# Short dummy matmuls at the start, one relu moved up, and the third batch's q scaled earlier in a fused attention and expert kernel

## The chip, the cores and the metric

The kernel runs on one core of one Trainium2 chip. The metric is the device time of one execution in microseconds (us), the median over several executions. Profiles are single executions; their clock starts at the first instruction of the program.

## The reference

```python
q_p = concat([relu(q) * cos, relu(q) * sin], -1)     # the same for k; cos and sin by position
kv  = einsum('bhsf,bhsd->bhfd', k_p, v); z = k_p.sum(2)
x   = einsum('bhsf,bhfd->bhsd', q_p, kv) / (einsum('bhsf,bhf->bhs', q_p, z) + 1e-6)
# x is laid out as 4608 x 512. Gates: exp(x @ w_gate), balanced 8 times over rows and columns
for e in range(8):
    out += P[:, e:e+1] * (relu(x @ w1[e]) @ w2[e])
```

There are 8 batches of 8 heads, 576 positions and 64 columns per head. Each expert is 512 by 1024 and 1024 by 512.

## The kernel before

The first phase works in blocks. Block j multiplies 512 tokens by the first expert's weights, slot by slot (slots 0 to 7 the first matrix, 8 to 15 the second). Between the slots it prepares the attention of a batch ahead: block 0 finishes batch 1 and starts batch 2 ("the third batch"), block 1 finishes batch 2, and so on. A helper, `at(block, slot, function, ...)`, puts a piece of work behind a slot. Three engines matter here: PE (TensorE), DVE (VectorE) and ACT (ScalarE). In these traces a piece that waits holds up what is written behind it on that engine: the k_p behind DVE's fourth scaling starts at 54.45 us in before, behind a wait of 1.91 us, and the first of four at 54.74 in after, behind one of 7.94 us (timelines below).

The parts that matter, abridged (`...` marks cuts):

```python
ld      = ...tile_pool(name="ld", bufs=4)        # loads of q, k, v: four half batches each
qp_pool = ...tile_pool(name="qp_pool", bufs=3)   # scaled q: three buffers

def keep_busy(n):                                # n * 128 columns of matmuls whose result is not used
    for cols in [512] * (n // 4) + [n % 4 * 128] * (n % 4 > 0):
        te.matmul(out=idle_ps[:, 0:cols], lhsT=ones_sq[:], rhs=..., start=True, stop=True)

def prep_q(b, hk):                               # two heads of batch b
    q16 = loaded.pop(("q", b, hk))
    if b >= 2: ve.tensor_scalar(out=q16, in0=q16, ..., op0=ALU.max)       # DVE relu
    q_p = qp_pool.tile([P, C, 2, D], F16, name="q_p")
    ve.tensor_tensor(out=q_p[:], in0=q16..., in1=cs, op=ALU.mult)         # DVE scaling
    if b >= 2:                                                            # turned by a DMA
        nc.sync.dma_start(out=qTs[b, hk], in_=q_p[:]..., transpose=True)
# prep_k: relu of k on ACT (b > 0); prep_kp: k_p, on DVE; prep_v: copy of v
# sums: k_p.T @ v on PE; denominators: PE, needs all four turned q; attend: the division
...
for hk in range(HK):                             # before block 0
    attend(0, hk)
    ...                                          # matmuls of slots 0 to 3, and for hk == 3 four relus on ACT
    for i in ((), (0,), (1, 2), (3,))[hk]: prep_k(1, i)
    for i in ((), (0,), (1,), (2, 3))[hk]: prep_kp(1, i)
...
# batch 2, as written: slots 12 to 15 of block 0, then slots 0, 1 and 3 of block 1
(12, prep_q, 0), (12, prep_k, 0), (13, prep_q, 1), (13, prep_k, 1),
(14, prep_kp, 0), (14, prep_v, 0, se.copy), (15, prep_kp, 1), (15, prep_v, 1, se.copy),
...
for hk in (2, 3):
    at(j, 0, prep_q, b, hk); at(j, 0, prep_k, b, hk)
    at(j, hk - 2, prep_kp, b, hk); at(j, hk - 2, prep_v, b, hk, se.copy)
at(j, 1, sums, b, 0); at(j, 3, sums, b, 1)
...
at(0, 3, load, 2, half); at(1, 0, load, 3, half)   # loads: the queue runs ahead of the slots
```

With three buffers for scaled q, the fourth scaling of a batch takes the buffer of its first. It waits until the first transposing DMA has landed (1.91 us in before; in b_bufs4, with a fourth buffer, not at all).

The softmax here doesn't subtract the row's maximum and nothing guards it: scores larger than these inputs give would overflow.

## Time and profile before

| what | before |
|---|---|
| time, median | 986.65 us (986.33 to 986.86, 4 runs) |
| first matmul of block 1 / of block 2 (timeline) | 48.03 us / 72.33 us |
| first transposing DMA: issued, landed | 46.09 us, 53.68 us |
| last load of batch 3 landed (trace record) | 52.65 us |

The page begins with the span and each engine's busy time and share:

```profile
span 985.4 us, 20168 instructions
## 1 busy us (share of the span) xinstructions
PE 967.8 (98%) x7817; PEld 671.3 (68%) x7817; DVE 805.8 (82%) x1829; ACT 566.7 (58%) x1267; POOL 60.6 (6%) x82
```

PE is nearly full, so what can be won are its holes. The view of waits for PE, from 8 to 75 us, says whom it waited for: total in us, how often, the longest.

```profile
PE small_ps L109 <- DVE k_p L109: 1.7, 1, 1.7
PE small_ps L109 <- DVE q_p L109: 1.6, 1, 1.6
PE small_ps L109 <- DMA q_pT<-q_p: 1.1, 1, 1.1
PE small_ps L109 <- issue: 0.9, 1, 0.9
PE h_ps L109 <- ACT hT L109: 0.6, 1, 0.6
```

"issue" means that nothing in the profile explains the wait. The chain that ended last, followed back through 40 to 62 us, has a start, a length and what was waited for on each line:

```profile
46.09 7.58 DMA q_pT<-q_p
53.68 0.03 issue
...
53.77 0.77 DVE q_p L109
...
54.62 4.59 DMA q_pT<-q_p
```

So the chain goes through the first transposing DMA, then the fourth scaling, then that one's own DMA. DVE's timeline (start, length, operation, and in brackets the idle time before it) shows the waiting instruction with its neighbours:

```profile
50.89 0.75 DVE L109 TENSOR_TENSOR k_p<-k_ld,acc_hi 128x1152 f16<-128x1152 f16 x1
51.56 0.30 DVE L109 TENSOR_SCALAR q_ld<-q_ld 128x576 f16<-128x576 f16 x1
53.77 0.76 DVE L109 TENSOR_TENSOR q_p<-q_ld,acc_hi 128x1152 f16<-128x1152 f16 x1 [1.91 <-DMA q_pT<-q_p]
54.45 0.75 DVE L109 TENSOR_TENSOR k_p<-k_ld,acc_hi 128x1152 f16<-128x1152 f16 x1
```

The last view is the table of busy time by stretch: busy us (and count) of PE, PEld, DVE, ACT and POOL, then the granted TensorE clock, DMA share and GB/s.

```profile
49.00:55.00 6.00, 3.98 (x67) 1.85 (x64) 4.05 (x8) 4.96 (x11) 0.00 (x0) 1.00 1.25 175
55.00:58.00 3.00, 2.75 (x44) 1.56 (x45) 0.85 (x5) 1.72 (x5) 0.00 (x0) 1.00 1.19 120
58.00:61.00 3.00, 1.90 (x37) 1.11 (x31) 1.33 (x2) 1.15 (x3) 0.00 (x0) 1.00 0.05 9
```

### The profile page before, as it was taken

The page shows a single profiled execution, that of the slowest core. Times are in us where ns is not written, and L with a number is a line of the kernel's source. Part 1 is how long each engine was busy: PE and PEld are TensorE (multiplying, and loading weights), DVE is VectorE, ACT ScalarE, POOL GpSimd, SP SyncE. Part 2 cuts the span into 40 slices and gives each one's busy share as a digit, 9 for nine tenths or more (in the row PEclk, how much of TensorE's full clock was granted, in tenths as well). Part 3 has the DMA queues.
Part 4 walks back from the last instruction along what each step waited for, and adds up shares of the span by engine and source line. Part 5 has one row for each costly group of instructions (what it writes and reads, how often), then busy time and mean ns, then how long its engine had stood idle before and what let it go on. Part 6 is the DMA issues. An engine that isn't in the chain of part 4 may idle for free.

```text
span 985.4 us, 20168 instructions
## 1 busy us (share of the span) xinstructions
PE 967.8 (98%) x7817; PEld 671.3 (68%) x7817; DVE 805.8 (82%) x1829; ACT 566.7 (58%) x1267; POOL 60.6 (6%) x82
## 2 busy tenths in 40 slices
PE   9889999989999999999999999999999999999997
PEld 4444544447777777777777777777777777777775
DVE  6676774789889888988789888988788888988887
ACT  5666665467776555555555555555555555555551
POOL 6311110010000000000000000000000000000001
PEclk9999999999999999999999999999999999999999
DMA  9979990641013410133103400233103401104435
GB/s 163 206 115 158 158 155 13 131 76 54 33 42 68 83 33 26 42 75 67 50 25 69 91 25 25 52 65 68 49 26 68 91 25 30 44 25 118 127 87 128
DMA packets 80336, 73.54 MB, mean 75 GB/s; under 512 B 33264, under 2 KB 72176, under 8 KB 80240
## 3 DMA queue, kind: packets, MB, share of 16 engines
q0 software_dynamic: 27232, 30.94, 19.9%
q1 hardware_dynamic: 52768, 41.06, 17.1%
q8 instruction: 61, 1.00, 0.4%
q14 instruction: 35, 0.29, 0.1%
q10 hardware_dynamic: 240, 0.26, 0.1%
HBM read 83.12 MB, written 12.98 MB: 98 GB/s over the span
## 4 chain that ended last, share of the span: by engine, by line
PE 94%; DVE 2%; ACT 2%; DMA 1%; issue 0%; POOL 0%; SPq 0%; ACTq 0%; DVEq 0%; POOLq 0%
PE rows_ps L109 34%; PE h_ps L109 27%; PE copied_ps L109 11%; PE p_ps L109 11%; PE y_ps L109 6%; PE small_ps L109 4%; DMA q_pT<-q_p 1%; ACT hT L109 0%; DVE acc_hi L904 0%; POOL hs_last L919 0%; DVE P_tok L109 0%; DMA out_dram<-acc_lo 0%; DVE colp L109 0%; ACT u L109 0%; ACT acc_lo L109 0%
## 5 line engine op out<-in xcount | busy, mean ns | idle before, releaser
L904 DVE SCALAR_TENSOR_TENSOR acc_lo<-rows_ps,P_tok,acc_lo 128x512 f32<-128x512 f32 (+1 forms) x322 | 203.9, 643 | 74.5 <-PE rows_ps L109 74.4
L109 PEld LDWEIGHTS <-H 128*128 128x128 f16 x2080 | 203.0, 98 | 83.1 <-issue 1.2
L840 ACT CAST u<-h_ps 128x384 f16<-128x384 f32 x288 | 137.6, 478 | 131.3 <-PE h_ps L109 131.3
L109 PEld LDWEIGHTS <-w1e 128*128 128x128 f16 x1632 | 156.4, 98 | 67.2 <-issue 6.9
L834 DVE CUSTOM_DVE_ANT_0 H<-p_ps,u 128x384 f16<-128x384 f32 x329 | 181.9, 553 | 7.0 <-PE p_ps L109 6.3
L109 PEld LDWEIGHTS <-hs 128*128 128x128 f16 x1500 | 146.5, 98 | 56.2
L109 PE MATMUL h_ps<-S,w1e 128*128 128x384 f16 x672 | 164.1, 326 | 1.1 <-ACT u L109 0.9
L109 PE MATMUL p_ps<-xT,T 128*128 128x384 f16 x672 | 164.1, 326 | 0.1
L109 PE MATMUL h_ps<-xT,w1e 128*128 128x384 f16 (+1 forms) x616 | 150.1, 350 | 0.8 <-ACT hT L109 0.6
L109 PE MATMUL rows_ps<-V,H 128*128 128x256 f16 x1000 | 150.0, 273 | 0.7 <-DVE acc_hi L904 0.7
L109 PE MATMUL rows_ps<-w2e,hs 128*128 128x256 f16 x1000 | 150.0, 273 | 0.0
L872 ACT ACTIVATE H<-h_ps 128x384 f16<-128x384 f32 x144 | 70.6, 490 | 95.1 <-PE h_ps L109 95.1
L109 PEld LDWEIGHTS <-T 128*128 128x128 f16 x1008 | 98.1, 98 | 29.3 <-issue 2.8
L109 PE MATMUL rows_ps<-w2e,H 128*128 128x256 f16 (+1 forms) x568 | 91.2, 285 | 0.0
L853 ACT COPY copied_ps<-h_ps 128x384 f32<-128x384 f32 x144 | 67.5, 469 | 35.3 <-PE h_ps L109 35.3
L863 ACT ACTIVATE H<-copied_ps 128x384 f16<-128x384 f32 x144 | 70.8, 492 | 20.4 <-PE copied_ps L109 20.4
L109 PE MATMUL h_ps<-S,T 128*128 128x384 f16 x336 | 81.8, 325 | 0.3 <-ACT copied_ps L109 0.3
L109 PE MATMUL copied_ps<-xT,w1e 128*128 128x384 f16 x336 | 82.1, 326 | 0.0
L109 PE MATMUL copied_ps<-w2e,H 128*128 128x256 f16 x504 | 75.5, 272 | 0.0
L109 PE MATMUL rows_ps<-V,hs 128*128 128x256 f16 x500 | 75.0, 272 | 0.0
L904 DVE SCALAR_TENSOR_TENSOR acc_lo<-copied_ps,P_tok,acc_lo 128x256 f32<-128x256 f32 x126 | 60.4, 480 | 0.4
L904 DVE SCALAR_TENSOR_TENSOR acc_hi<-rows_ps,P_tok,acc_hi 128x512 f32<-128x512 f32 (+1 forms) x56 | 41.4, 739 | 19.9 <-PE rows_ps L109 19.1
(147 smaller groups left out, 952.4 us busy)
## 6 DMA issues: line engine op xcount, KB each, us to landing
S<-x_saved SPq DMA_DIRECT2D x108, 192.0 KB, 2.4
out_dram<-acc_lo SPq DMA_DIRECT2D x62, 128.0 KB, 2.4
w1e<-in_moe_w_dram POOLq DMA_DIRECT2D x7, 1024.0 KB, 9.0
w2e<-in_moe_w_dram POOLq DMA_DIRECT2D x7, 1024.0 KB, 10.1
q_ld<-in_q_dram POOLq DMA_DIRECT2D x16, 288.0 KB, 7.5
k_ld<-in_k_dram POOLq DMA_DIRECT2D x16, 288.0 KB, 8.9
v_ld<-in_v_dram POOLq DMA_DIRECT2D x16, 288.0 KB, 9.4
x_saved<-S SPq DMA_DIRECT2D x18, 192.0 KB, 1.9
```

What stands on the lines that cost most here:

```text
L109: i = getattr(self.engine, name)(*args, **kwargs)
L834: latest = ve._custom_dve(TENSOR_ADD_SAT, out=out, in0=ps[:, 0:TU], in1=t[:], s0=FP32_MAX, s1=0.0)
L840: se.copy(out=t[:], in_=ps[:, 0:TU])
L853: se.copy(out=Y[:, 0:TU], in_=X[:, 0:TU])
L863: se.activation(out=h11, in_=Y[:, 0:TU], func=AF.Relu)
L872: se.activation(out=h12, in_=X[:, 0:TU], func=AF.Relu)
L904: ve.scalar_tensor_tensor(out=a, in0=rows, scalar=P_tok[:, g, self.e : self.e + 1], in1=a, op0=ALU.mult, op1=ALU.add,)
```

## The change

There are three parts, to which the rest of this text refers.

- *Dummies*: the first 80 dummy units are issued as 80 matmuls of 128 columns instead of 20 of 512.
- *Relu*: ACT's relu of k(1,3) stands ahead of four relus of the expert's hidden layer, so that k_p and q_p of batch 1 come sooner.
- *Order*: all four scalings of batch 2's q move into block 0 (from slot 8 on), so that their transposing DMAs start sooner. The keys and values of batch 2 follow as the first work of block 1, and its attends start at slot 9.

```diff
-        keep_busy(80)
+        for _ in range(80):
+            keep_busy(1)
@@
-        def prep_k(b, hk):
+        def prep_k(b, hk, by_scalar=True):
-            if b:
+            if b and by_scalar:
@@
             attend(0, hk)
+            if hk == 3:
+                prep_k(1, 3)
@@
-            for i in ((), (0,), (1, 2), (3,))[hk]:
+            for i in ((), (0,), (1, 2), ())[hk]:
                 prep_k(1, i)
@@  block 1
-                    for hk in (2, 3):
-                        at(j, 0, prep_q, b, hk)
-                        at(j, 0, prep_k, b, hk)
-                        at(j, hk - 2, prep_kp, b, hk)
-                        at(j, hk - 2, prep_v, b, hk, se.copy)
-                    at(j, 1, sums, b, 0)
-                    at(j, 3, sums, b, 1)
+                    for hk in range(HK):
+                        if hk >= 2:
+                            at(j, 0, prep_k, b, hk, False)
+                        at(j, 0, prep_kp, b, hk)
+                        at(
+                            j, (0, 0, 1, 3)[hk], prep_v, b, hk,
+                            (ve.tensor_copy, se.copy)[hk // 2],
+                        )
+                    at(j, 3, sums, b, 0)
+                    at(j, 5, sums, b, 1)
@@
-                at(j, 5 if j == 1 else 3, denominators, b)
+                at(j, 6 if j == 1 else 3, denominators, b)
                 for hk in range(HK):
-                    at(j, (8 if j == 1 else 6) + 2 * hk, attend, b, hk)
+                    at(j, (9, 10, 12, 13)[hk] if j == 1 else 6 + 2 * hk, attend, b, hk)
@@  block 0
-                    (12, prep_q, 0), (12, prep_k, 0), (13, prep_q, 1), (13, prep_k, 1),
-                    (14, prep_kp, 0), (14, prep_v, 0, se.copy), (15, prep_kp, 1),
-                    (15, prep_v, 1, se.copy),
+                    (8, prep_q, 0), (11, prep_k, 0), (12, prep_q, 1), (12, prep_k, 1),
+                    (13, prep_q, 2), (14, prep_q, 3),
```

(The slots of batch 3's preparation in block 1 are rearranged too; that list is cut here.)

## The prediction

> **What bounds the kernel now.** The page gives PE 967.8 of 985.4 us busy (98%), and the chain that ended last is 94% PE: time can only come from where PE stands still. The change touches the first 72 us. The table by stretch shows PE full from 60 to 180 us, but not before (6.62 of 10 us in 50 to 60). The timeline shows PE's holes:
> - 30.15 us: 1.6 us, transposes of batch 1 wait for q_p; DVE had waited 2.46 us for ACT's relu of k(1,3), queued behind four hidden relus.
> - 34.0 and 34.6 us: 0.32 and 0.21 us; ACT is nearly full there.
> - 52.1 us: 0.57 us (ACT hT); 55.26: 1.70 us (k_p of batch 2); 59.25: 1.10 us (last transposing DMA). The chain of waits has 7.58 us DMA q_pT from 46.09, a DVE q_p, then 4.59 us DMA q_pT: with three q_p buffers the fourth scaling waits for the first transpose.

> **Parts, costed.**
> 1. 80 dummies of 128 columns for 20 of 512: same columns. Weight loads come 0.42 us apart until 6.24 us, then about 0.21. [...] That moment should stay; with more weight loads (nine warm 128-column pairs took 0.68 us) the dummies end 0.2 to 0.6 us later. Keys land at 10.7 us anyway. Cost 0 to 0.3 us.
> 2. ACT's k(1,3) before the four relus: k_p and q_p of batch 1 come 2 us earlier, the 1.6 us hole closes, then ACT limits. Gain 1.3 us.
> 3. Batch 2's q from slot 8 (DVE idles near 41 us): first transpose 5 us earlier, no 4.59 us tail. The 3.4 us of holes close in part. Given back: block 1 starts with about 4.4 us of DVE work (two relus 0.30, four k_p 0.75, two copies 0.45) behind the last q_p; the sums at slot 3 need v(2,1): PE waits 0.5 to 1.8 us. DMA is saturated till 52 us (205 GB/s), so the first transpose may take 7 us again and hold the fourth scaling 1.5 us. DVE has about 21 us of work in block 1 against PE's 20.2: 0.3 to 0.8 us of wait moves to batch 3's sums. Net gain 1.5 us.

> From 60 us PE is full, and later holes (180 to 220 us, sinkhorn) follow work that moves along: the gain is kept.

> **Prediction.** 986.6 - 1.3 - 1.5 + 0.1 = 983.9 us; 8 in 10: 981.8 to 986.3. Faster by over 2%: 0.01; within 2%: 0.98; slower by over 2%: 0.01.

> **What would show each step right.**
> - Dummies: first transposes at 8.7 to 9.1 us (before 8.54), first DVE zsel at most 0.3 us after 12.39.
> - k(1,3): q_p of batch 1 starts near 27 us (before 29.34), no PE wait for it; sums of batch 1 1 to 1.5 us earlier.
> - First transposing DMA at 40 to 42 us (before 46.09), last landed before 58 (59.2); PE's waits in 48 to 60 us 1 to 2.5 us, on k_p or v of batch 2.
> - Block 2's first matmuls 2 to 3.5 us earlier (before 72.33), everything later shifted the same.

> **What would make it wrong.** If transposes starve behind the loads, the fourth q_p blocks DVE 4 us or more: no gain, or a loss. If short dummies leave the array cold longer, the start loses 1 us or more. If neither, and DVE keeps up, the gain is 4 to 5 us. The compiler may also order loads differently.

## The result

The changed kernel takes 990.04 us (989.82 to 990.27, 4 runs) against 986.65 us. The ratio is 1.0035, with a 95% interval of 1.0017 to 1.0052. Ratios here are the mean time of one kernel's fast runs over that of the other's of the same rounds, so they are not quite the ratio of the quoted medians. The change is a loss of 3.4 us, clear of noise, and the time lies outside the predicted range.

```profile
span 988.3 us, 20283 instructions
## 1 busy us (share of the span) xinstructions
PE 969.5 (98%) x7877; PEld 676.3 (68%) x7877; DVE 807.0 (82%) x1833; ACT 565.3 (57%) x1263; POOL 60.6 (6%) x82
```

The page hardly differs; the loss is in one place. PE's waits from 8 to 75 us:

```profile
PE small_ps L109 <- DVE acc_lo L109: 7.6, 3, 6.9
PE small_ps L109 <- ACT acc_lo L109: 0.2, 1, 0.2
PE small_ps L109 <- ACT acc_hi L109: 0.2, 1, 0.2
PE h_ps L109 <- DVE xT L109: 0.2, 1, 0.2
```

The waits for q_p, k_p, the DMA and "issue" that were listed before are gone. In their place stands one hole of 6.9 us. (The name acc_lo here is the space that is lent to the copies of v.) The chain from 40 to 62 us shows what is behind it:

```profile
39.69 14.29 DMA q_pT<-q_p
...
54.07 0.76 DVE q_p L109
54.83 0.67 DVE k_p L109
55.49 0.36 DVE acc_lo L109
55.86 0.67 DVE k_p L109
56.52 0.37 DVE acc_lo L109
```

The first transposing DMA was issued 6.4 us sooner than before, at 39.69 instead of 46.09. It landed at 53.97, which is 0.3 us later than before. DVE's timeline shows the cost:

```profile
45.83 0.30 DVE L109 TENSOR_SCALAR q_ld<-q_ld 128x576 f16<-128x576 f16 x1
54.07 0.76 DVE L109 TENSOR_TENSOR q_p<-q_ld,acc_hi 128x1152 f16<-128x1152 f16 x1 [7.94 <-DMA q_pT<-q_p]
54.74 0.75 DVE L109 TENSOR_TENSOR k_p<-k_ld,acc_hi 128x1152 f16<-128x1152 f16 x1
```

The fourth scaling waited 7.94 us instead of 1.91, and now all four k_p of batch 2 stand behind it. The table by stretch has a second effect in its column of clocks (the seventh after the stretch's length):

```profile
49.00:55.00 6.00, 0.00 (x0) 0.00 (x0) 0.93 (x2) 1.16 (x2) 0.00 (x0) 0.91 1.25 187
55.00:58.00 3.00, 1.74 (x38) 1.31 (x39) 2.97 (x7) 0.38 (x2) 0.00 (x0) 0.50 0.66 132
58.00:61.00 3.00, 3.00 (x10) 0.91 (x10) 2.12 (x6) 0.66 (x2) 0.00 (x0) 0.54 0.00 0
```

While PE stood idle the array's clock was halved, and it stayed halved after work came back. The trace's clock record has one spell of 6.83 us at 0.5 there (53.96 to 60.78 us), and none there in before. PE's hole is 6.94 us (48.97 to 55.91).

The balance, from the two timelines: block 1 starts 2.71 us earlier (45.32 instead of 48.03), and block 2 starts 3.05 us later (75.38 instead of 72.33). So block 1 takes 5.76 us more. After 75 us PE's larger holes (over 0.25 us) add up to 4.24 us in before and in after: the later parts neither gave nor took.

### The profile page after: what moved, and what is told of

Its sections match the earlier page's. It is cut to its first block, busy times and chain, and to the rows that moved or that the text cites. A ratio compares the mean times of both kernels' runs of the same rounds, so it can differ in the third digit from the quotient of the medians.

```text
span 988.3 us, 20283 instructions
## 1 busy us (share of the span) xinstructions
PE 969.5 (98%) x7877; PEld 676.3 (68%) x7877; DVE 807.0 (82%) x1833; ACT 565.3 (57%) x1263; POOL 60.6 (6%) x82
## 3 DMA queue, kind: packets, MB, share of 16 engines
q1 hardware_dynamic: 52768, 41.06, 16.9%
## 4 chain that ended last, share of the span: by engine, by line
PE 93%; DVE 2%; ACT 2%; DMA 2%; POOL 0%; issue 0%; ACTq 0%; SPq 0%; DVEq 0%; POOLq 0%
PE rows_ps L109 34%; PE h_ps L109 27%; PE copied_ps L109 11%; PE p_ps L109 11%; PE y_ps L109 6%; PE small_ps L109 4%; DMA q_pT<-q_p 1%; ACT hT L109 0%; DVE acc_hi L913 0%; POOL hs_last L928 0%; DVE P_tok L109 0%; DMA out_dram<-acc_lo 0%; DVE colp L109 0%; ACT u L109 0%; ACT acc_lo L109 0%
```

## The experiments

Two theories of the transposing DMA were set against each other.

- *Drain theory*: issued while loads are queued, it lands only when those loads have drained, near 54 us, whenever it was issued.
- *Own-time theory*: it takes its time from its issue (7.6 us before, 14.3 us after), so a later issue means a later landing.

Of the gains in front there was a second pair: *additive* (an earlier start of block 1 is kept, as I had predicted) against drain (it is swallowed by a landing that does not move).

The twelve new kernels gave correct results, and every one was run with a profile and in three timed rounds beside the kernel before on the same chip. Landings are the trace's own records, in us. The column of loads gives the last landing of the loads that are in flight with the transpose. In after, b_filled, b_q3_after_keys and b_bufs4 the last of these was issued 0.5 to 1.2 us behind the transpose (at 40.84 in after), in the other runs ahead of it.

| kernel | time, median | ratio (95% interval) | first transpose: issued, landed | last load landed | DVE wait at 4th scaling |
|---|---|---|---|---|---|
| before (profile) | 986.65 | | 46.09, 53.68 | 52.65 | 1.91 |
| after (profile) | 990.04 | 1.0035 (1.0017 to 1.0052) | 39.69, 53.97 | 53.96 | 7.94 |
| a_dummies | 987.02 | 0.9999 (0.9984 to 1.0014) | 45.65, 52.22 | 51.07 | 0.89 |
| a_relu | 987.63 | 1.0009 (0.9994 to 1.0023) | 44.04, 53.30 | 52.52 | 3.58 |
| a_dummies_relu | 988.72 | 1.0020 (1.0005 to 1.0035) | 43.92, 55.24 | 53.04 | 5.64 |
| a_order | 989.51 | 1.0027 (1.0010 to 1.0044) | 42.27, 53.33 | 52.85 | 4.82 |
| b_q0_late | 989.20 | 1.0024 (1.0009 to 1.0039) | 43.86, 53.05 | 52.27 | 5.68 |
| b_q3_after_keys | 985.54 | 0.9989 (0.9973 to 1.0006) | 39.63, 54.82 | 54.86 | 4.83 |
| b_filled | 988.80 | 1.0021 (1.0006 to 1.0036) | 38.87, 53.59 | 53.69 | 8.37 |
| b_loads_held | 983.40 | 0.9968 (0.9951 to 0.9984) | 39.47, 44.39 | 43.18 (batch 2's) | none |
| b_bufs4 | 987.08 | 0.9999 (0.9984 to 1.0014) | 40.20, 53.67 | 53.69 | none |
| a_dummies256 | 985.52 | 0.9983 (0.9966 to 1.0000) | 45.47, 53.23 | 52.29 | 2.08 |
| c_held_bufs4 | 984.62 | 0.9979 (0.9956 to 1.0002) | 39.14, 44.19 | 43.02 (batch 2's) | none |
| c_held_less | 990.54 | 1.0035 (1.0020 to 1.0050) | 39.34, 44.62 | 43.36 (batch 2's) | none |

### The three parts by themselves

a_dummies is before with the dummies alone:

```diff
-        keep_busy(80)
+        for _ in range(80):
+            keep_busy(1)
```

> Before with the short dummies alone. Drain theory (the first transposing DMA of batch 2 lands only when the loads in flight have drained, at 53.5 to 54 us, whenever it was issued, and the fourth scaling waits for it): block 1 starts about 0.9 us earlier, because the hole of 0.91 us without a releaser at 16.9 us is gone as in after, but the landing stays at 53.5 to 54 and the time stays at 986.3 to 986.9. Additive theory (PE's earlier start is kept): 985.6 to 985.9. My prediction: 986.7.

Measured: the hole of 0.91 us is gone, but block 1 starts only 0.44 us earlier (47.59), because this profile began worse: its array came up to full clock at 7.05 us, against 6.26 in before, and its first transposes on PE start at 9.02 us, against 8.54. The first transpose was issued at 45.65 us. The time is no better: 987.02 us median, 984.50 to 987.77. The lowest run is the profiled one. It had clock 1.000, its loads landed 1.6 us sooner than in before (51.07), and its transpose landed 1.15 us behind them (52.22), sooner than either theory had said. The other three runs had clock 0.997 and took 986.99 to 987.77. No gain is shown; one run in four suggests that there is one where the clock holds.

a_relu is before with the relu alone:

```diff
             attend(0, hk)
+            if hk == 3:
+                prep_k(1, 3)
...
-            for i in ((), (0,), (1, 2), (3,))[hk]:
+            for i in ((), (0,), (1, 2), ())[hk]:
```

> Before with the relu of k(1,3) moved ahead of the four hidden relus, alone. Drain theory: block 1 starts 1.5 to 1.8 us earlier (before 48.03), first transposing DMA issued as much earlier, landing still at 53.5 to 54, time 986.3 to 986.9. Additive theory, which my prediction used: 984.8 to 985.3.

Measured: 987.63 us, ratio 1.0009. PE's wait of 1.6 us for q_p is gone, as designed. The landing stays at 53.30, PE's wait for batch 2's k_p grows from 1.70 to 3.38 us, and the clock is halved for 6.83 us. The additive theory's 985 is out. The drain theory's 986.9 was passed too, since it had left the clock out.

a_dummies_relu has both early parts.

> Both early parts without the new order of batch 2. Drain theory: block 1 starts near 45.3 us, landing of the first transpose still 53.5 to 54.1, time 986.2 to 986.9. Additive theory: 983.8 to 984.2.

Measured: 988.72 us, ratio 1.0020, so slower than before by more than noise. PE's hole is 5.43 us and the clock is halved for 6.83 us. Two improvements of the start, with the schedule of batch 2 untouched, make the kernel slower: PE arrives sooner at a wait that ends no sooner, and the one long hole halves the clock, a cost that the profile of before does not have. In this run the transpose landed 2.2 us behind the last load, which my expectation did not cover.

a_order is after without the other two parts:

```diff
-        for _ in range(80):
-            keep_busy(1)
+        keep_busy(80)
...
-            if hk == 3:
-                prep_k(1, 3)
...
-            for i in ((), (0,), (1, 2), ())[hk]:
+            for i in ((), (0,), (1, 2), (3,))[hk]:
```

> After without the short dummies and with the relu of k(1,3) back in its place: the new order of batch 2 alone. Drain theory: block 1 starts near 48 us, but the fourth scaling still waits till about 54, so the time is that of after, 989.7 to 990.3, or up to 1.7 less because a hole that starts later is too short to halve the clock. Additive theory (2.7 us of early gain lost again): 992.4 to 993.

Measured: 989.51 us. The additive theory's 992.4 is out. The hole of 3.82 us was not too short: the clock was halved for 6.83 us, as in after. The new order makes the loss with or without the early parts; in after, the 2.7 us of earlier start bought nothing.

### The transposing DMA: drain or its own time

b_q0_late issues the first transpose later:

```diff
-                    (8, prep_q, 0), (11, prep_k, 0), ...
+                    (11, prep_k, 0), (12, prep_q, 0), ...
```

> After with the first scaling at slot 12, so the first transpose is issued near 42 to 43.5 us instead of 39.69. Drain theory: it lands at 53.5 to 54.2 all the same; time within 0.4 of after. Own-time theory (14.3 us from issue to landing): it lands at 56 to 58 and the time is 2 to 4 us over after.

Measured: issued 4.2 us later than in after (43.86), landed 0.9 us earlier (53.05), just behind the last load (52.27). The ratio, 1.0024, is not worse than after's 1.0035; the time misses "within 0.4" on the fast side. The own-time theory is refuted.

b_loads_held takes the loads away from the transposes: batch 3's loads are issued after the fourth scaling instead of running ahead.

```diff
-                    at(1, 0, load, b + 2, half)
+                    at(0, 15, load, b + 2, half, "qkv", True)    # True: behind DVE's last instruction
```

> After with batch 3's loads issued only after the fourth scaling of batch 2. Drain theory: batch 2's loads drain near 43.6 us, the first transpose lands by 46.5 instead of 54.0, the fourth scaling starts before 47.5, PE's hole of 6.9 us is gone, the clock stays whole; time 981 to 984 (batch 3's data come later and may cost some of it). Own-time theory (a transposing DMA issued here takes some 14 us whatever else moves): landing still near 54, time 990 or more.

Measured: 983.40 us, ratio 0.9968 (0.9951 to 0.9984). The first transpose landed at 44.39, 1.2 us behind the last load of batch 2. DVE's timeline has no wait at the fourth scaling (second line), and the keys follow at once:

```profile
45.62 0.30 DVE L109 TENSOR_SCALAR q_ld<-q_ld 128x576 f16<-128x576 f16 x1
45.95 0.76 DVE L109 TENSOR_TENSOR q_p<-q_ld,acc_hi 128x1152 f16<-128x1152 f16 x1
46.63 0.75 DVE L109 TENSOR_TENSOR k_p<-k_ld,acc_hi 128x1152 f16<-128x1152 f16 x1
```

This is the test of the cause. The change of after is kept whole and only the competing loads are moved. The loss of 3.4 us becomes a gain of 3.35 us (983.40 against 986.75 for the kernel before, measured beside it).

The later runs qualify the drain theory. In b_loads_held the fourth transpose was issued at 46.80, just ahead of batch 3's first load (47.01). It landed at 53.15, beside that load (53.31) and long before the batch had drained (61.74). In c_held_less the fourth was issued at 46.85, behind three loads of batch 3 and ahead of three, and landed at 62.06, with the last of all six (61.88). In after, too, the load it landed with was issued 1.15 us behind it. So a transpose can also land with loads that are issued just behind it. Which loads hold it is not shown.

How it lands so late in after can be split with the trace's packets. In the trace the transpose is 1152 packets of 256 bytes. The trace does not say which DMA a packet belongs to; counted in the order of their start, the first starts at 43.67 us, 3.98 us after the issue, and the 1152nd ends at 51.38. The landing is recorded at 53.97. The three stretches are 3.98, 7.71 and 2.59 us; for batch 3's first transpose in before, which meets no load, they are 1.17, 1.52 and 0.65 us. The profile's DMA view for 43 to 51 us of after shows the two queues side by side (packets, MB, share of 16 engines):

```profile
q0 software_dynamic: 1214, 1.31, 95.2%
q1 hardware_dynamic: 1050, 0.27, 24.7%
```

q0 holds the loads, q1 the transposes. From 44 to 50 us, 146 transposing packets and 140 load packets of 1152 bytes ended per microsecond: about as many of one kind as of the other, so the transposes got only a fifth of the bytes (37 of 198 KB per microsecond). What sets these counts is not shown. The landing is recorded at 53.97, 0.01 us behind the last load's 53.96 and 2.59 us behind the 1152nd packet. What these 2.59 us wait for no run here isolates, nor the 3.98 us ahead of the first packet.

### The place of the fourth scaling, and the buffer

b_q3_after_keys leaves the landing late, but puts the waiting instruction behind the keys:

```diff
-                    (13, prep_q, 2), (14, prep_q, 3),
+                    (13, prep_q, 2),
...
+                    at(j, 0, prep_q, b, 3)          # block 1, behind all prep_kp of slot 0
                     at(j, 3, sums, b, 0)
```

> After with the fourth scaling behind batch 2's keys and values in DVE's order. Head-of-line theory (the landing is as late as before, what costs is that everything queues behind the one DVE instruction that waits for it): first landing still near 54, but the first sums of batch 2 run near 49.5 us instead of 55.9, the wait moves to the denominators (fourth transpose lands near 58.5); PE's hole shorter than 5 us; time 984 to 987. If the hole had another cause: 989 to 991.

Measured: 985.54 us (984.47 to 987.88), ratio 0.9989. The landing is as late as ever (54.82), but PE's longest hole is 3.8 us instead of 6.9, and the median is 4.5 us below after's (measured in other rounds). So the loss of after needs both: the late landing, and the keys written behind the instruction that waits for it.

b_bufs4 takes the wait away with a fourth buffer:

```diff
-        qp_pool = ...(name="qp_pool", bufs=3)
-        rb_pool = ...(name="rb_pool", bufs=4)
+        qp_pool = ...(name="qp_pool", bufs=4)
+        rb_pool = ...(name="rb_pool", bufs=3)       # for space
```

> After with a fourth q_p buffer (and three rb buffers instead of four, for space). Drain theory: the first transpose still lands near 54 us, but the fourth scaling waits for nothing and runs near 47 us; the keys follow; all four transposes land one after the other at 54 to 58 us, and PE's one wait is that of the denominators, until 57 to 58 us; its hole is 3 to 4.5 us and may or may not reach the half clock. Time 983.5 to 986.5, at least 3.5 under after. If another thing than the buffer held DVE: hole of 6.9 us stays, time 989 to 991.

Measured: 987.08 us, ratio 0.9999; 0.6 us above the upper end of the expectation, and 2.96 us under after's median where at least 3.5 had been expected. The fourth scaling waits for nothing, and the first transpose lands at 53.67 as before. PE's waits from 40 to 75 us are one line:

```profile
PE small_ps L109 <- DMA q_pT<-q_p: 3.2, 3, 2.0
```

The wait has moved to the denominators, which need all four transposes (the fourth landed at 58.12). The clock is halved for 3.41 us. Between 177 and 981 us this kernel also lost 0.48 us against before, as did both c kernels with the same buffers; why was not looked into.

### What the half clock costs

b_filled is after with dummy matmuls inside the hole:

```diff
+                    if fn is sums and (j, slot) == (1, 3):
+                        idle_ps = ps_y.tile([P, Dm], FP32, name="y_ps")
+                        keep_busy(112)
                     fn(*args)
```

> After with 28 dummy matmuls of 512 columns (6.05 us at full clock) put into PE's hole before the first sums of batch 2. Same waits, but the array is not idle: granted clock 1.000 instead of 0.997, the eight 512-column matmuls after the hole take 1.9 us instead of 3.48; time 1.3 to 2 us under after, 988 to 988.7. If the lower clock costs nothing because DVE limits there: within 0.3 of after.

Measured: 988.80 us (988.16 to 990.02), ratio 1.0021 against after's 1.0035, so 1.4 us by the ratios; the median misses the range by 0.1 us. The eight matmuls behind the hole, first of after, then of b_filled:

```profile
57.55 3.48 PE L109 MATMUL h_ps<-xT,w1e 128*128 128x512 f16 x8
```

```profile
56.94 1.90 PE L109 MATMUL h_ps<-xT,w1e 128*128 128x512 f16 x8
```

From the third slot of block 1 to the third slot of block 2, after took 30.81 us (47.09 to 77.90) and b_filled 29.44 us (46.27 to 75.71), 1.37 us less. The half clock is then about 1.4 us of the 5.8 us that block 1 lost, and the wait itself is the rest. The two were measured in different rounds, and the interval of the ratio is as wide as the difference, so this share is an estimate from one profile each and the two ratios. It may be low: b_filled's fourth scaling waited 0.43 us longer than after's (8.37 against 7.94).

### The hole without a cause

In before PE stood 0.91 us in the middle of the sums of batch 0, released by nothing in the profile. In after it is gone, and I had not foreseen it. a_dummies256 issues 40 dummies of 256 columns:

```diff
-        keep_busy(80)
+        for _ in range(40):
+            keep_busy(2)
```

> Before with 40 dummies of 256 columns: 20 pairs of a weight load and a matmul more than before, where 80 of 128 have 60 pairs more. Fetch theory (the hole of 0.9 us without a releaser in the sums of batch 0 lies at a fixed count of PE instructions[...]): the hole is still there, 20 pairs earlier in the 72 pairs of the sums, so after about 28 of them instead of 48; block 1 starts as in before, near 48 us, and the time is 986 to 987. Theory that shorter dummies as such feed the start better (my prediction had them cost 0.1 us): the hole is smaller in proportion or gone as with 128 columns.

The sums are 72 matmuls, each with a weight load. PE's timeline of before, of a_dummies256, and of after:

```profile
16.00 0.88 PE L109 MATMUL small_ps<-v_ld,k_p 64*128 64x64 f16 x48
17.78 0.53 PE L109 MATMUL small_ps<-v_ld,k_p 64*128 64x64 f16 x24 [0.91 <-issue]
```

```profile
15.56 0.58 PE L109 MATMUL small_ps<-v_ld,k_p 64*128 64x64 f16 x28
16.87 0.82 PE L109 MATMUL small_ps<-v_ld,k_p 64*128 64x64 f16 x44 [0.73 <-issue]
```

```profile
15.99 1.22 PE L109 MATMUL small_ps<-v_ld,k_p 64*128 64x64 f16 x72
```

Twenty more pairs at the start move the hole twenty pairs forward, from 48 to 28, exactly as expected: in these two profiles it lies at the same count of PE instructions. The trace has a 16,384-byte packet of the instruction queue ending at 16.15 us in before, at 15.48 in a_dummies256 and at 13.03 in after. From such packets the theory has its name; that the hole waits for one was my estimate, and it is not shown: the packet ended 0.7 us before the hole began (16.88 in before, 16.14 in a_dummies256), and the next four such packets of before, ending at 22.53, 38.55, 44.53 and 57.71 us, come with no hole of this kind. Nor is it known why the hole is gone with 60 more pairs. The times (985.52 us, 985.29 to 986.96) were expected at 986 to 987 and are 0.5 us better; with an interval that touches 1.0000 I draw nothing from that.

### A version that beats both

c_held_bufs4 joins b_loads_held and b_bufs4. c_held_less is the same, with the loads released after the third scaling:

```diff
-                    at(0, 15, load, b + 2, half, "qkv", True)
+                    at(0, 13, load, b + 2, half, "qkv", True)
```

> b_loads_held with the fourth q_p buffer: candidate to beat both. In b_loads_held the fourth scaling of batch 3 waited 2.65 us for a transpose that landed among batch 3's late loads, and PE stood 1.41 us at 64 us; with four buffers that wait goes. Time 981.5 to 983, 0.5 to 1.5 under b_loads_held.

> c_held_bufs4 with the loads of batch 3 released after the third scaling, some 1.7 us earlier. If late data of batch 3 still cost time in c_held_bufs4 (DVE waited 2.26 us for q_ld in b_loads_held): 0.3 to 1.2 us faster than it. If the fourth transpose, now among the loads, costs as much: the same within 0.4 or slower.

Measured: c_held_bufs4 took 984.62 us (982.74 to 988.18), 1.6 us above the expected range. The run with clock 1.000 was the fastest and the run with 0.996 the slowest. It is not shown better than b_loads_held (the intervals of both overlap). In its profile a hole of 2.07 us at 53.5 us is followed by 3.41 us of half clock, which b_loads_held does not have. c_held_less took 990.54 us. That is the "or slower" branch of its expectation, by far more than the 0.4 us named there, and the drain theory should have told me so. Its fourth transpose was issued at 46.85, behind three of batch 3's six loads; the last of the six landed at 61.88, and the transpose at 62.06. PE's timeline at the denominators:

```profile
62.10 0.51 PE L109 MATMUL small_ps<-q_pT,zsel 128*32 128x192 f16 x6 [8.18 <-DMA q_pT<-q_p]
```

Releasing the loads 1.5 us sooner (first issue 45.15 instead of 46.68 us) cost 5.9 us. The best kernel by its ratio is b_loads_held, 0.32% faster than before. With the loads out of the way the changed kernel falls into the predicted range (983.40 against 983.9 predicted). That fits a prediction that failed at this one wait, but the near hit is partly luck, since moving the loads shifts batch 3's work too: in b_loads_held PE stood 1.41 us at 62.61, which after has not.

## Why the prediction was wrong

- **The step that failed** is in part 3: "the first transpose may take 7 us again and hold the fourth scaling 1.5 us". It took 14.29 us and held it 7.94 us. I read 46.09 to 53.68 as a duration, but it was the time that was left until the loads had drained (last landing 52.65). Eleven profiled kernels with that queue in place issued the first transpose between 38.9 and 46.1 us; all landed between 52.2 and 55.2 us. In these kernels an earlier issue had no earlier end.
- **"The gain is kept"** failed for the same reason. The relu part did what was said (q_p of batch 1 at 25.86 us, no PE wait for it), and block 1 of after starts 2.71 us sooner. But a_relu and a_dummies_relu show no gain from an earlier start (ratios 1.0009 and 1.0020).
- **The clock** was missing from the sum for part 3. With the hole of 6.94 us it was halved for 6.83 us; filling the hole gave about 1.4 us back.
- **"PE's waits in 48 to 60 us 1 to 2.5 us, on k_p or v of batch 2"** named the right place (v's copies, behind the scaling), but the wait was 7.3 us.
- **Part 1** was mis-sized, at the start with the wrong sign. The dummies' end hardly moved (next matmuls at 8.15 instead of 8.09 us), and the hole of 0.91 us went away. Its first signs, transposes at 8.61 us and zsel (DVE's tile for the denominators) at 12.46 us, are about as said, 0.1 us sooner for the first. But that says little: over the fourteen profiles the first transposes start between 7.77 and 9.07 us, the latest where the array came up to full clock last (3.86 to 7.16 us, whatever the kernel). Before and after happen to lie close together (6.26 and 6.17 us; in before the dummies of 512 columns start 0.43 us apart until then and 0.22 us apart behind it).
- **What would make it wrong** was named: "If transposes starve behind the loads, the fourth q_p blocks DVE 4 us or more: no gain, or a loss". That is what happened. I gave it too little weight, although the trace of before already held the evidence: the transpose and the last load landed within 1.1 us of each other.

## What to carry to other kernels

Before moving the start of a transfer forward, ask what its end depends on. Here first transposes issued from 38.9 to 46.1 us, with batch 3's loads in flight, all landed between 52.2 and 55.2 us: the length in the profile (7.58 us in before, 14.29 in after) was only the distance to that moment, and the loads had to move instead (b_loads_held: 983.40 us). An instruction that may wait for a late event belongs behind the work that others need from the same engine (b_q3_after_keys: 985.54 us, against 990.04 for after). And a gain ahead of a wait that ends no sooner did not only vanish: it lengthened the hole (from 1.70 to 3.38 us in a_relu), and each of the seven holes of 3.38 us or more in these traces came with a halved clock.
